# Attention and gated FFN on one core: output rows of the later batches stored as one transfer for each 32 rows

## The chip, the cores and the metric

The kernel runs on one core of one Trainium2 chip. The metric is the device time of one execution, in microseconds (us); lower is better. The kernel before took 1076.05 us (median of three runs, 1075.31 to 1076.84). The profile is of a separate execution that took 1074.98 us, of which the recorded span, from the first instruction to the last, is 1073.2 us.

Engine names in the profile: PE is the matrix engine (PEld its weight loads), DVE the vector engine, ACT the scalar engine, POOL the GpSimd engine. SP is the sync engine; it computes nothing and issues DMA transfers. A name with a q at its end (SPq, ACTq) is an engine's instruction queue: the issue of a transfer, or a wait. L498 means line 498 of the kernel's file.

## The reference

Two stages. A linear attention without softmax (8 batches, 8 heads, 576 positions, head size 64), each head's output row divided by its root mean square; then a gated feed-forward layer over all 4608 rows of 512 numbers.

```python
kv  = np.einsum('bhsd,bhse->bhde', k, v)
out = np.einsum('bhsd,bhde->bhse', q, kv)
rms = np.sqrt(np.mean(out * out, axis=-1, keepdims=True) + 1e-06)
x   = (out / rms * g_norm).transpose(0, 2, 1, 3).reshape(4608, 512)
gate = 1.0 / (1.0 + np.exp(-(x @ w_gate)))     # 512 -> 1536
val  = x @ w_val
y    = gate * val @ w_out                      # 1536 -> 512
```

The output is 4608 rows of 512 float32 numbers, 2 KB a row, 9.44 MB in all.

## The kernel before

The rows are worked on in nine chunks of 512 rows (c = 0 to 8). A chunk goes through a first layer (gate and value), then a second layer. While chunk c is in its first layer, the attention of batch c+1 is fed into the free slots between its matrix products. All tensors are float32.

The chunk's rows don't stand in memory order. Attention leaves the positions of a batch in an order that suits its transposes, and the store puts them back. For batches 0 and 1 the rows of a tile go to every sixth row of the output, in runs of up to 96. For batches 2 to 7 the order is finer: position s = 192 r + 6 p + 2 g + i, with p from 0 to 31. A group of 32 neighbouring rows of a tile has one (i, r, g) and all 32 p; up to three groups with the same i and r follow each other.

```python
QB = 32; NJ = 6; JH = NJ // 2; XC = QB * JH     # XC = 96
def sg_tile():
    return sb.tile([P, G], FP32, tag="sg", name="sg", bufs=5)     # five buffers, [128, 512]

def store(c, t, ot, cols=slice(0, DM), queues=(nc.sync,)):
    r0 = i = 0
    while r0 < P:                                     # P = 128 rows of the tile ot
        b, s = divmod(G * c + P * t + r0, S)
        rows = out[S * b:S * b + S, cols]
        if b < 2:
            j, p = divmod(s, NP)
            n = min(P - r0, NP - p)
            queues[i % len(queues)].dma_start(        # L492
                out=rows.rearrange("(p j) d -> j p d", j=NJ)[j, p:p + n], in_=ot[r0:r0 + n, cols])
        else:
            half, c0 = divmod(s, S // 2)
            r, c0 = divmod(c0, XC)
            n = min(P - r0, XC - c0)                  # 32, 64 or 96 rows
            queues[i % len(queues)].dma_start(        # L498
                out=rows.rearrange("(r p g i) d -> i r g p d", p=QB, g=JH, i=2)[
                    half, r, c0 // QB:(c0 + n) // QB],
                in_=ot[r0:r0 + n, cols])
        r0 += n
        i += 1
```

A 128-row tile so takes two transfers (96 and 32 rows, or 64 and 64). The second layer of a chunk ends with its four stores and then, on the same queue (SP), the loads of k and v for the batch that is two ahead. The tiles that are stored come from the same five buffers as those that the first layer of the next chunk writes:

```python
def second_layer_fast(c):                             # chunks 1 to 7
    ...                                               # (cut: products, L893 and L952)
    store(c, 2, o2[0])
    split(o1, d1, a2, sa2, b2, tw2_, lambda: store(c, 3, o2[1]))
    for g in pair:
        store(c, g, o1[g])
    load_late(c + 2)                                  # L114, L119: k and v, then used by feed

def first_layer_fast(c):
    ...
        def p1_out(d):
            d["u"] = d["sg"] = sg_tile()
            nc.scalar.copy(out=d["sg"][:, h2], in_=d["pa"])   # L741, on ACT
        ...
            small(pd[:, q1], tw2[2], s2[:, 1], False)
            nc.scalar.copy(out=g2[:, q1], in_=pd[:, q1])      # L801, on ACT
            small(one["pa"][:, q2], tw2[4], ax[:, 1, q2], False)   # L732, on PE

def feed(b):
        def kv_mm():                                  # L354, L360, on PE: the first use of k and v
            ...
```

Chunk 8 has a second layer of its own (L1003) in two rounds, g = 0 and 1. In the second its result is stored by column parts as they become ready, the last two parts of 128 columns over both issuing engines:

```python
            store(c, 2 + g, o2)                       # 128 x 512
            ...
            for (i_c, pc), x in zip(pcs, parts):      # parts: two of 128 columns
                give(i_c)
                product(pc, lambda f: s4[c, f][:, t1], b[2, 2][:, :, x], False)
                y = slice(DH + x.start, DH + x.stop)
                tt(out=o1[:, y], in0=pc, in1=o1[:, y], op=ALU.add)      # L1037, on DVE
                if last:
                    store(c, g, o1, y, (nc.sync, nc.scalar))
```

The framework gives every transfer one of eight completion semaphores in turn. A transfer waits, before it is issued, until the one that had its semaphore before has landed.

Of the kernel before, what the change touches and what calls it, by code (L numbers as in the profile page):

```python
# [20 lines left out]
def kernel(  # L21
# [16 lines left out]
    P = 128  # L38
# [3 lines left out]
    JH = NJ // 2  # L42
# [8 lines left out]
    QB = 32  # L51
# [3 lines left out]
    XC = QB * JH  # L55
# [427 lines left out]
    def store(c, t, ot, cols=slice(0, DM), queues=(nc.sync,)):  # L483

        r0 = i = 0
        while r0 < P:
# [5 lines that stand above are left out]
                queues[i % len(queues)].dma_start(out=rows.rearrange("(p j) d -> j p d", j=NJ)[j, p:p + n],  # L492
                                                  in_=ot[r0:r0 + n, cols])
            else:
                half, c0 = divmod(s, S // 2)
                r, c0 = divmod(c0, XC)
                n = min(P - r0, XC - c0)
                queues[i % len(queues)].dma_start(  # L498
                    out=rows.rearrange("(r p g i) d -> i r g p d", p=QB, g=JH, i=2)[half, r, c0 // QB:(c0 + n) // QB],
                    in_=ot[r0:r0 + n, cols])  # L500
            r0 += n
            i += 1
# [97 lines left out]
    for token in order.split():  # L600
        name = token.rstrip("0123456789.")
        n = [int(i) for i in token[len(name):].split(".")]
# [283 lines left out]
    def second_layer_fast(c):  # L886
# [95 lines left out]
        split(o2, d1, a4, sa4, b4, tw4)  # L982
# [5 lines that stand above are left out]
# [90 lines left out]
    for c in range(1, NG):  # L1078
        if c + 1 < B:
            steps = feed(c + 1)  # L1080
            if c == 1:

                i = 4
# [38 lines left out]
```

## Time and profile before

| | |
|---|---|
| time, median of 3 | 1076.05 us |
| span of the profile | 1073.2 us |
| PE busy | 1058.8 us, 99% |
| DVE, ACT, POOL busy | 69%, 29%, 55% |
| stores of L498 | 56 on SP, 2 on ACT |
| stores of L492 | 18 on SP |
| issue of one L498 store on SP | 0.32 to 2.26 us, median 0.70 us |
| last operation that computes | begins at 1065.46 us, takes 0.29 us |

The profile has several views. The page gives busy time by engine and the granted clock of PE in 40 slices (9 in every one: full speed). The chain of waits follows the work that ended last back in time: at each step to what released it. The list of waits tells which engine stood still and what ended it. The timeline lists instructions by start. A transfer has two times: how long its issue held the engine's queue, and when it landed, that is, when its completion semaphore was full.

### The profile page before, as it was taken

Reading aid. Unit: us, or ns where it says so; the run is one execution under the profiler, and the core shown is the slowest. Engines: PE = TensorE matmul, PEld = TensorE weight load, DVE = VectorE, ACT = ScalarE, POOL = GpSimd, SP = SyncE. Lnnn points to the kernel's source line nnn. Section 1 sums busy time; section 2 is a strip of 40 time slices with the busy share of each in tenths; the row PEclk is TensorE's granted clock in tenths of the full one; section 3 lists DMA queues with packets and bytes.
Section 4 is the critical chain, followed back from the end, with each engine's and each line's share of the span. In section 5 each row is a group of like instructions: output and inputs, shape, how many; then the busy total and the mean of one; then the engine's idle time right before and its main releaser. Section 6 shows DMA issues by size and latency. Waiting matters only on the chain.

```text
span 1073.2 us, 20591 instructions
## 1 busy us (share of the span) xinstructions
PE 1058.8 (99%) x7766; PEld 887.6 (83%) x7766; DVE 740.8 (69%) x1545; ACT 308.0 (29%) x737; POOL 587.6 (55%) x966
## 2 busy tenths in 40 slices
PE   9999999999999999999999999999999999999997
PEld 8544448888988888889888988889888988898886
DVE  4887767995678557874778557956787478738841
ACT  4654323231233113330333124311432122102210
POOL 0000036877367917783668537792778277847700
PEclk9999999999999999999999999999999999999999
DMA  9944710002400231012301140024001200010001
GB/s 271 242 157 157 244 29 23 13 13 56 140 12 13 54 103 41 23 35 48 114 13 42 28 139 13 14 55 118 22 24 25 52 10 1 1 27 14 1 1 39
DMA packets 69122, 65.03 MB, mean 61 GB/s; under 512 B 23712, under 2 KB 63008, under 8 KB 69024
## 3 DMA queue, kind: packets, MB, share of 16 engines
q1 hardware_dynamic: 68768, 63.69, 21.0%
q8 instruction: 62, 1.02, 0.4%
q14 instruction: 36, 0.29, 0.1%
q10 hardware_dynamic: 256, 0.03, 0.1%
HBM read 47.19 MB, written 9.44 MB: 53 GB/s over the span
## 4 chain that ended last, share of the span: by engine, by line
PE 95%; DMA 4%; SPq 0%; issue 0%; ACT 0%; DVE 0%; ACTq 0%
PE mm L728 45%; PE mm L893 17%; PE mm L556 7%; PE mm L732 7%; PE mm L952 5%; PE mm L653 4%; PE mm L1003 3%; DMA out_dram<-sg 3%; PE at L395 2%; PE at L354 1%; PE at L556 1%; PE two L261 1%; DMA kv<-in_v_dram 1%; PE two L291 0%; DMA v<-in_v_dram 0%; PE mm L634 0%
## 5 line engine op out<-in xcount | busy, mean ns | idle before, releaser
L720 POOL TENSOR_TENSOR tw<-gv 128x256 f32<-128x256 f32 x192 | 158.7, 836 | 258.6 <-DVE w L202 144.6
L728 PE MATMUL mm<-xT,tw 128*128 128x256 f32 x768 | 199.5, 382 | 0.0
L728 PE MATMUL mm<-sx,tw 128*128 128x256 f32 x768 | 197.5, 380 | 0.0
L720 POOL TENSOR_TENSOR tw<-gv,tw 128x256 f32<-128x256 f32 x192 | 153.5, 819 | 0.0
L728 PEld LDWEIGHTS mm<-xT,tw 128*128 128x128 f32 x768 | 136.6, 190 | 19.4 <-issue 3.8
L728 PEld LDWEIGHTS mm<-sx,tw 128*128 128x128 f32 x768 | 134.9, 191 | 12.4
L808 POOL TENSOR_TENSOR sg<-sg 128x256 f32<-128x256 f32 x48 | 35.1, 732 | 168.5 <-ACT sg L807 168.5
L775 DVE TENSOR_TENSOR gv<-gv,sg 128x256 f32<-128x256 f32 x192 | 110.9, 596 | 0.0
L741 ACT COPY sg<-mm 128x256 f32<-128x256 f32 x96 | 36.0, 375 | 248.8 <-PE mm L728 242.1
L728 PE MATMUL mm<-xT,gv 128*128 128x256 f32 x384 | 90.8, 379 | 0.0
L728 PE MATMUL mm<-sx,gv 128*128 128x256 f32 x384 | 90.7, 379 | 0.0
L766 ACT ACTIVATE sg<-sg 128x256 f32<-128x256 f32 x96 | 39.9, 415 | 149.5 <-DVE sg L765 149.4
L728 PEld LDWEIGHTS mm<-sx,gv 128*128 128x128 f32 x384 | 73.0, 190 | 9.9
L728 PEld LDWEIGHTS mm<-xT,gv 128*128 128x128 f32 x384 | 72.3, 190 | 10.0 <-issue 0.5
L556 PE MATMUL mm<-xT,gv 128*128 128x512 f32 x176 | 77.4, 594 | 0.0
L893 PE MATMUL mm<-w,s 128*128 128x256 f32 x336 | 73.7, 379 | 0.0
L893 PEld LDWEIGHTS mm<-w,s 128*128 128x128 f32 x336 | 63.8, 190 | 8.7
L751 DVE TENSOR_TENSOR gv<-mm,sg 128x256 f32<-128x256 f32 x96 | 40.0, 416 | 42.2 <-PE mm L728 41.3
L556 PEld LDWEIGHTS mm<-xT,gv 128*128 128x128 f32 x176 | 32.6, 190 | 37.4 <-issue 35.9
L747 DVE TENSOR_TENSOR gv<-mm,sg 128x256 f32<-128x256 f32 x96 | 36.6, 412 | 39.1 <-PE mm L728 32.1
L765 DVE TENSOR_TENSOR sg<-mm,sg 128x256 f32<-128x256 f32 x96 | 40.5, 421 | 33.0 <-PE mm L728 32.9
L713 POOL TENSOR_TENSOR tx<-gv,tx 128x128 f32<-128x128 f32 x96 | 54.6, 568 | 7.5
(156 smaller groups left out, 1908.5 us busy)
## 6 DMA issues: line engine op xcount, KB each, us to landing
q<-in_q_dram SPq DMA_DIRECT2D x24, 288.0 KB
st<-in_moe_w_gate_dram SPq DMA_DIRECT2D x12, 512.0 KB
st<-in_moe_w_val_dram SPq DMA_DIRECT2D x12, 512.0 KB
st<-in_moe_w_out_dram SPq DMA_DIRECT2D x12, 512.0 KB
kv<-in_k_dram SPq DMA_DIRECT2D x24, 256.0 KB
kv<-in_v_dram SPq DMA_DIRECT2D x24, 256.0 KB
out_dram<-sg SPq DMA_DIRECT2D x23, 192.0 KB
xT<-xTs SPq DMA_DIRECT2D x48, 72.0 KB
```

Of the source, the lines that this page charges most:

```text
L556: nc.tensor.matmul(self.ps[i], w[("wg", "wv")[i], self.f][:, m, :], xT[self.c][:, m, :], start=(m == 0), stop=(m == NMT - 1), skip_group_c ...
L653: nc.tensor.matmul(ps[t], gv[0, f][:, P * t:P * t + P], w["wo", f], start=(f == 0), stop=(f == NFT - 1), skip_group_check=True)
L713: nc.gpsimd.tensor_tensor(out=tw2[i], in0=in0, in1=tw2[in1] if isinstance(in1, int) else in1, op=ALU.subtract)
L720: nc.gpsimd.tensor_tensor(out=tw[f, i], in0=b[in0], in1=b[in1] if isinstance(in1, tuple) else tw[f, in1], op=ALU.subtract)
L728: nc.tensor.matmul(ps, wt[:, m, :], xs[:, m, :], start=(new and m == 0), stop=(m == NK - 1), skip_group_check=True)
L732: nc.tensor.matmul(ps, wt, xs, start=new, stop=True, skip_group_check=True)
L751: tt(out=d["h"][:, h2], in0=ps, in1=d.pop("u")[:, h2], op=ALU.add)
L765: tt(out=d["sg"][:, h2], in0=d["pb"], in1=d["sg"][:, h2], op=ALU.add)
L766: nc.scalar.activation(out=d["sg"][:, h2], in_=d["sg"][:, h2], func=AF.Sigmoid)
L775: tt(out=d["h"][:, h], in0=d["h"][:, h], in1=d["sg"][:, h], op=ALU.mult)
L893: nc.tensor.matmul(ps, hs[f], ws[:, f, :], start=(new and f == 0), stop=(f == NF2 - 1), skip_group_check=True)
L952: nc.tensor.matmul(ps, hs[j], ws[j], start=(new and j == 0), stop=(j == N3 - 1), skip_group_check=True)
```

## The change

The second branch of the store always takes one group of 32 rows. A 128-row tile of batches 2 to 7 so takes four transfers of 32 rows instead of two of 32 to 96. On both sides of a transfer the outermost dimension is now 32 rows; before, that of the output side was the number of groups, 2 or 3. The bytes, their places in memory and the order of the tiles stay as they were.

```diff
             else:
+
                 half, c0 = divmod(s, S // 2)
                 r, c0 = divmod(c0, XC)
-                n = min(P - r0, XC - c0)
+                n = QB
                 queues[i % len(queues)].dma_start(
-                    out=rows.rearrange("(r p g i) d -> i r g p d", p=QB, g=JH, i=2)[half, r, c0 // QB:(c0 + n) // QB],
+                    out=rows.rearrange("(r p g i) d -> i r g p d", p=QB, g=JH, i=2)[half, r, c0 // QB],
                     in_=ot[r0:r0 + n, cols])
             r0 += n
             i += 1
```

No instruction of PE, DVE or POOL is added, removed or moved. L498 is line 499 in the changed kernel, and so on below it.

## The prediction

> **What bounds the kernel now.** I read the page first: busy times, then the chain that ended last.
>
> ```profile
> PE 1058.8 (99%) x7766; PEld 887.6 (83%) x7766; DVE 740.8 (69%) x1545; ACT 308.0 (29%) x737; POOL 587.6 (55%) x966
> ...
> PE 95%; DMA 4%; SPq 0%; issue 0%; ACT 0%; DVE 0%; ACTq 0%
> PE mm L728 45%; PE mm L893 17%; PE mm L556 7%; PE mm L732 7%; PE mm L952 5%; PE mm L653 4%; PE mm L1003 3%; DMA out_dram<-sg 3%; PE at L395 2%; PE at L354 1%; PE at L556 1%; PE two L261 1%; DMA kv<-in_v_dram 1%; PE two L291 0%; DMA v<-in_v_dram 0%; PE mm L634 0%
> ```
>
> PE bounds the kernel. A change that touches no product can win only from the 1073.2 - 1058.8 = 14.4 us in which PE does nothing. That total caps the gain. But the chain shows stores, "out_dram<-sg", with 3%, so some of the 14.4 us belongs to them. Where do they lie? The timeline of the end comes next (start, duration, engine, line; the number before x is a count).
>
> ```profile
> 1062.58 2.84 PE L1003 MATMUL mm<-w,s 128*128 128x128 f32 x24
> ...
> 1063.23 3.25 SPq L498 DMA_DIRECT2D out_dram<-sg  x4
> ...
> 1064.44 1.66 ACTq L498 DMA_DIRECT2D out_dram<-sg  x2
> 1065.46 0.29 DVE L1037 TENSOR_TENSOR sg<-mm,sg 128x128 f32<-128x128 f32 x1 [1.05 <-PE mm L1003]
> ```
>
> All computing ends at 1065.75 (1065.46 + 0.29), the span at 1073.2: a tail of 7.45 us in which only the last stores land. Inside the kernel, PE's gaps after the start-up (longer than 0.1 us) are seven: 0.39, 1.13, 0.59, 0.96, 0.51, 0.50 and 0.22 us, together 4.3 us. The chain names what ended the larger ones (start, duration, what). Around 385 us:
>
> ```profile
> 385.38 8.54 DMA out_dram<-sg
> 393.92 0.03 ACTq L741
> 393.94 0.04 issue
> 393.99 0.37 ACT sg L741
> 394.36 0.18 ACT sg L801
> ```
>
> and around 624 us:
>
> ```profile
> 624.42 10.82 DMA out_dram<-sg
> 635.24 0.02 issue
> 635.26 0.02 SPq L114
> 635.28 0.03 issue
> 635.30 5.67 DMA kv<-in_v_dram
> ```
>
> A store that takes 8.54 us keeps one of the five sg buffers; ACT cannot write it, and PE waits 1.13 us for ACT. A store of 10.82 us keeps a completion semaphore, so the last large v load is issued only at 635.30. PE needs k and v from 638.95 on and stands for 0.96 + 0.51 us. The same happens as at 385 us once more at 739.75 (0.50 us). ACT's and PE's own lines say it:
>
> ```profile
> 393.99 0.37 ACT L741 COPY sg<-mm 128x256 f32<-128x256 f32 x1 [2.63 <-DMA out_dram<-sg]
> ...
> 394.58 0.49 PE L732 MATMUL mm<-xT,tx 128*128 128x128 f32 x2 [1.13 <-ACT sg L801]
> ```
>
> So late stores cost PE 1.13 + 0.96 + 0.51 + 0.50 = 3.1 us inside, and up to 7.45 us at the end.
>
> **What the Trainium skill says.** "DMA: Bandwidth & Descriptors", section "Why a DMA increments its semaphore by 16 and not by 1": a transfer issued by SP or ACT is not always spread over all 16 DMA engines. The outermost dimension (not of size 1) of each side is taken, and the largest number up to 16 that divides both is the number of engines; they are the lowest-numbered ones. For a store of three groups the output side has 3 outermost and the tile side 96, so 3 engines; for two groups 2; for one group 32 and 32, so 16. The same section says that the issuing side writes 16 minus that number to the semaphore at once and each engine adds one. The trace agrees: among the semaphore updates it records, every three-group store has 4 updates, every two-group store 3 and every single-group store 16. The landing times agree too. Counted from the end of issue to the last update, a three-group store of full rows takes 5.58 us at least, one of two groups 4.71, one of a single group 1.28. It also explains why a single-group store is sometimes slow (median 6.53 us): its packets stand behind the long ones on the lowest engines. The same page's section "Queues, rings and completion order" says that on each engine the queue is worked off in order. The trace shows this: a store of 32 rows issued at 615.88 landed at 622.26, 0.18 us after the three-group store issued before it.
>
> **The change part by part.** In the program, the transfers of the later batches go from 58 to 116, each with a third or half of the bytes, or the same. No compute instruction moves.
>
> 1. Issue on SP. Where nothing delays it, the issue of a single group takes 0.32 us, of two 0.53, of three 0.73, and 0.05 us pass between two. A 128-row tile costs 0.32 + 0.05 + 0.73 = 1.10 us before and 4 x 0.32 + 3 x 0.05 = 1.43 us after. That is 0.33 us more a tile and 1.3 us more a chunk of four. SP is seldom on the chain, and this lies under PE's work except at the very end.
>
> 2. Landing of the stores inside. Single groups over 16 engines should land about 1.3 to 1.9 us after issue, in place of 5 to 11. The semaphore of a store is then free long before its next turn: eight issues at 0.37 us take 3.0 us, more than 0.32 + 1.3. The sg buffer that ACT wanted at about 391.4 and got at 393.9 was stored by a transfer issued at 385.38; it should be free by about 388. The wait for it goes, and with it 1.13 and 0.50 us on PE. The stores of the chunk around 620 us finish issuing at about 623 (the last DVE addition ends at 619.75 by the timeline, then eight single stores at 0.37 us) instead of 625.16, and the k and v loads neither queue behind stores nor wait for their semaphores. In the trace, once the stores had drained, these loads landed one each 0.7 us. Eight of them and four small ones should land by about 632, well before 637.80, where PE first wants them. So 0.96 + 0.51 us go. Sum inside: 3.1 us. The remaining gaps (0.39, 0.59, 0.22) have no store in their cause and I leave them.
>
> 3. The tail. The last tile of four groups is ready at 1065.75. Before, one store of 96 x 128 numbers over three engines was issued in 0.70 us, landed at 1072.19 and 1.0 us later the span ended. It was late less because of its own bytes than because of the three-group store of full rows at 1063.60, which landed at 1070.57 on the same engines. After: both SP and ACT issue two single stores, 0.32 + 0.05 + 0.32, ready at 1066.46. SP has at 1063.23 four stores of full rows to issue and then two of the first part; that ends at about 1063.23 + 6 x 0.37 = 1065.45, before the last part is ready. Landing after 1.3 us: 1067.8. The same 1.0 us to the end: 1068.8 in place of 1073.2. Gain 4.4 us.
>
> Sum: 4.4 + 3.1 = 7.5 us. I take 0.5 us off, because something else often waits just behind a wait that is removed. 1076.05 - 7.0 gives **1069.0 us**.
>
> **The rivals.** First, SP becomes the hindrance: twice as many issues, all ahead of the k and v loads on one queue. For it: the loads came late at 638.95, and 1.3 us more a chunk is as large as the gaps. Against it: SP spent up to 2.26 us on issuing one single-group store while the queues were full (at 622.11), seven times what it takes when free; most of its time is such waiting. If landings did not improve, five chunks would lose up to 1.3 us each and the time would be about 1080. Second, eight completion semaphores for sixteen stores a chunk: if each still took 7 us to land, sixteen would take two rounds of 7 us, and the k and v loads would be several us later in five chunks, 1080 to 1090. The 1.28 us of a lone single-group store speaks against it. Third, the writes are limited by memory and not by the spread: then nothing moves, 1076. Against it: a 128-row tile in two and three groups moved at about 60 GB/s in the tail, while the first of the page's 40 slices reaches 271. Fourth, the inside gains nothing, since gaps are replaced by others (the x rows through SP, the vector engine), and only the tail wins: 1071.6.
>
> **Range and chances.** Both parts full: 1068.5. Only the tail: 1071.6. A tail somewhat shorter still, and PE's small delays below 0.1 us also gone: 1067. The runs before scatter by 0.8 us to each side. The range is 1067.0 to 1072.3. Faster by over 2% would mean below 1054.5, more than all of the 14.4 us that PE is not busy: chance 0.01. Slower by over 2% would need the semaphore rival at its worst, over 1097: 0.01. Within 2%: 0.98.
>
> **What would show it.** After, all stores of L499 should have 16 semaphore updates and land within about 2 us; the chain should no longer have 8 us pieces of "out_dram<-sg"; the wait of ACT L741 for a store (6.2 us over six times) should vanish; the gaps at about 393, 639 and 740 us should close; and the end should follow the last DVE operation by about 3 us instead of 7.45. I am wrong if landing stays near 7 us, if SP's issue time between the end of a second layer and the first k load grows beyond 3.5 us and the k and v gap widens, or if new gaps open in the first layer.

## The result and the profile after

The changed kernel took 1067.55 us (median of four runs, 1066.82 to 1069.17), the kernel before, measured with it, 1076.44 us (four runs). The ratio is 0.9918, with a 95% interval from 0.9899 to 0.9937: 8.9 us less. The predicted time was 1069.0 us and the range 1067.0 to 1072.3.

The first thing to look at is again the chain of waits on the page, here of the changed kernel (shares of the span by engine, then by line):

```profile
span 1066.2 us, 20718 instructions
...
PE 98%; DMA 1%; SPq 1%; issue 0%; DVE 0%
PE mm L729 47%; PE mm L894 17%; PE mm L557 7%; PE mm L733 7%; PE mm L953 6%; PE mm L654 4%; PE mm L1004 3%; PE at L395 2%; PE at L354 1%; DMA v<-in_v_dram 1%; PE at L557 1%; PE two L261 0%; PE two L291 0%; PE two L318 0%; PE two L272 0%; SPq L87 0%
```

"out_dram<-sg", 3% before, is gone from the chain, and so are the k and v loads of the later batches. What is left of DMA in it is the first v load of the start. The chain begins at the last operation that computes, so the tail is not in it: the 3% before were three landings inside (8.54, 10.82 and 7.97 us), and PE worked through most of that time. The timeline of ACT where it waited 2.63 us for a buffer (start, duration; in brackets the idle time before and what ended it):

```profile
391.52 0.37 ACT L742 COPY sg<-mm 128x256 f32<-128x256 f32 x1 [26.47 <-PE mm L729]
392.61 0.27 ACT L795 COPY sg<-mm 128x128 f32<-128x128 f32 x1 [0.71 <-PE mm L733]
392.77 0.38 ACT L742 COPY sg<-mm 128x256 f32<-128x256 f32 x1
393.92 0.27 ACT L802 COPY sg<-mm 128x128 f32<-128x128 f32 x1 [0.77 <-PE mm L733]
```

The second copy of L742 now has no bracket: its buffer was free. Here ACT only waits for PE, and in the list of all its waits no store is left (6.2 us, six times before). PE at the first use of k and v:

```profile
637.71 2.08 PE L354 MATMUL at<-kv 128*64 128x64 f32 x64
639.73 0.46 PE L360 MATMUL at<-kv 64*64 64x64 f32 x16
640.12 1.13 PE L729 MATMUL mm<-xT,tw 128*128 128x256 f32 x4
```

All 64 products run in one piece. And the end:

```profile
1060.36 3.68 SPq L499 DMA_DIRECT2D out_dram<-sg  x8
1061.24 0.29 DVE L1038 TENSOR_TENSOR sg<-mm,sg 128x128 f32<-128x128 f32 x1 [0.91 <-PE mm L1004]
1061.57 2.13 ACTq L499 DMA_DIRECT2D out_dram<-sg  x4
1062.59 0.29 DVE L1038 TENSOR_TENSOR sg<-mm,sg 128x128 f32<-128x128 f32 x1 [1.05 <-PE mm L1004]
```

Computing ends at 1062.88 us and the span at 1066.2. All 116 changed stores have 16 semaphore updates in the trace. Those of full rows land 1.28 to 2.86 us after the end of their issue (median 1.29), where the three-group stores took 5.58 to 10.30 us and the two-group ones 4.71 to 10.85.

To see where the time comes from, I cut the span at four places that a reader can find by line: the start of the second layer of chunk 0, the start of the first layer of chunk 2, the start of the second layer of chunk 8 ("inside" is between the last two), and the end of the last DVE operation ("tail" is from there to the end). All in us.

| kernel | second layer of chunk 0 begins | inside | tail |
|---|---|---|---|
| before | 118.11 | 754.42 | 7.45 |
| changed | 119.58 | 750.13 | 3.34 |
| e1, last chunk only | 118.24 | 753.99 | 3.10 |
| e2, chunks 2 to 7 only | 122.16 | 750.64 | 7.31 |
| e3, 16 and 16 rows | 120.08 | 757.71 | 7.63 |
| e4, 17 and 15 rows | 118.93 | 780.99 | 9.61 |
| e5, tiles 0 and 1 only | 118.05 | 754.19 | 7.25 |
| e6, tile 2 only | 118.75 | 750.06 | 7.71 |
| e7, loads first | 118.84 | 764.80 | 7.45 |
| e8, last tile over both queues | 118.85 | 749.92 | 3.14 |

So the changed kernel gains 754.42 - 750.13 = 4.3 us inside and 7.45 - 3.34 = 4.1 us at the end, together 8.4 us. The two profiles differ by only 7.0 us (1073.2 and 1066.2) because the changed kernel's profiled execution happened to be about 1.4 us slower before anything that is changed. The first column shows that this part differs from run to run by up to 4 us with the same program up to there.

### The profile page after: what moved, and what is told of

It reads as the page before. It is cut to its first block, busy times and chain, and to the rows that moved or that the text cites. A ratio compares the mean times of both kernels' runs of the same rounds, so it can differ in the third digit from the quotient of the medians.

```text
span 1066.2 us, 20718 instructions
## 1 busy us (share of the span) xinstructions
PE 1058.0 (99%) x7766; PEld 887.8 (83%) x7766; DVE 740.6 (69%) x1545; ACT 307.2 (29%) x737; POOL 587.5 (55%) x966
## 4 chain that ended last, share of the span: by engine, by line
PE 98%; DMA 1%; SPq 1%; issue 0%; DVE 0%
PE mm L729 47%; PE mm L894 17%; PE mm L557 7%; PE mm L733 7%; PE mm L953 6%; PE mm L654 4%; PE mm L1004 3%; PE at L395 2%; PE at L354 1%; DMA v<-in_v_dram 1%; PE at L557 1%; PE two L261 0%; PE two L291 0%; PE two L318 0%; PE two L272 0%; SPq L87 0%
## 5 line engine op out<-in xcount | busy, mean ns | idle before, releaser
L742 ACT COPY sg<-mm 128x256 f32<-128x256 f32 x96 | 36.0, 375 | 242.7 <-PE mm L729 238.8
```

## The experiments

All ratios are to the kernel before, with 95% intervals. The edits are to the kernel before unless said otherwise.

**e1 and e2: the two halves alone.**

```diff
-                n = min(P - r0, XC - c0)
+                n = QB if c == NG - 1 else min(P - r0, XC - c0)   # e1
+                n = QB if c < NG - 1 else min(P - r0, XC - c0)    # e2
```

> Only the stores of the last chunk (c = 8) go 32 rows at a time; chunks 2 to 7 store as before. My theory: the gain has two parts that don't touch each other. The tail from the end of the last DVE operation to the end of the span falls from 7.4 us to about 3.3 us, the gaps of PE at about 393, 639 and 740 us stay, and the time is 4.1 us under the kernel before: about 1072.3 us. Rival that the tail alone carries the gain (the gaps inside would be replaced): the whole 8.9 us, about 1067.5.

> Only the stores of chunks 2 to 7 go 32 rows at a time; the last chunk stores as before. My theory: the gaps of PE at about 393, 639 and 740 us close, worth about 4.3 us between the first layers of chunks 2 and 8; the tail stays at about 7.4 us; about 1072 us. Rival that the tail alone carries it: 1076, no gain.

e1 took 1070.35 us, ratio 0.9956 (0.9942 to 0.9970); e2 1071.22 us, ratio 0.9959 (0.9947 to 0.9971). The shortfalls from 1 add up to 0.44% + 0.41% = 0.85% (4.7 and 4.4 us, where I had expected 4.1 and 4.3); the whole change has 0.82%. In e1 the tail is 3.10 us and PE's gaps at about 393, 639 and 740 us are still there (1.09, 0.64 + 0.63 and 0.50 us). In e2 these are closed and the tail is 7.31 us. The two parts are separate and of about the same size; the rival that the tail carries all is out.

**e3 and e4: what makes a store fast, its size or its spread.** Both cut each 32-row group in two. The number of transfers is the same, and their sizes differ by one row.

```diff
-                n = min(P - r0, XC - c0)
+                n = 16 if c0 % QB == 0 else QB - c0 % QB          # e3; in e4: 17
...
-                    ...i=2)[half, r, c0 // QB:(c0 + n) // QB],
+                    ...i=2)[half, r, c0 // QB, c0 % QB:c0 % QB + n],
```

> Each group of 32 rows is cut once more, into transfers of 16 and 16 rows: eight transfers a tile, each with a number of rows that 16 engines divide. My theory: every store has 16 semaphore updates and still lands within about 2 us of its issue, but SP now issues 32 stores a chunk at about 0.47 us, so the first k load goes out about 7 us later than with 32-row stores and PE stands for k and v for 1 to 3 us in some of the five chunks; the tail grows by about 1 us. About 1069 to 1078 us, so roughly as before or a little better. Rival that a smaller transfer is what makes stores fast: better than the changed kernel, under 1067.

> The same number of transfers and almost the same sizes as with 16 and 16 rows, but 17 and 15: 17 is divided by no number up to 16 but 1, 15 by 15. My theory (the spread over DMA engines decides): a 17-row store has 2 semaphore updates, one of 15 rows 16; one engine carries 18 of each 32 rows and the stores of a tile land only after some 10 us, those of a chunk after 30 us or more; loads of k and v queue behind them on that engine, and PE stands for them in each of five chunks. Over 1100 us, with a tail of over 15 us. Rival (number and size of the transfers decide, not their spread): within 2 us of the 16 and 16 kernel.

e3 took 1078.0 us, ratio 1.0025 (1.0015 to 1.0034), e4 1105.34 us, ratio 1.0282 (1.0262 to 1.0303). Between the two the only difference is one row more here and less there, and it costs 27 us. In e3 every store has 16 updates, and those of full rows land 1.23 to 3.29 us after the end of their issue (median 1.25, with 32 rows 1.29). In e4 the 17-row stores have 2 updates (one from the issuing side, one from an engine), and those of full rows land at a median of 5.56 us. The chain of waits of e4 after the second layer of chunk 4 shows how they pile up (start, duration, what):

```profile
629.11 5.95 DMA out_dram<-sg
635.06 0.02 issue
635.08 5.79 DMA out_dram<-sg
640.87 0.02 issue
640.88 5.79 DMA out_dram<-sg
646.67 0.02 issue
646.69 5.81 DMA out_dram<-sg
```

Each link is a store that waits for the landing of the one eight before it, which has its semaphore. One pair of 17 and 15 rows lands each 1.45 us (636.50, 637.96, 639.42 and so on). The Trainium skill ("DMA: Bandwidth & Descriptors", section "Why a DMA increments its semaphore by 16 and not by 1") gives 1 engine to the one and 15 to the other, the lowest-numbered ones, so the first engine carries 18 rows of 2 KB of each pair: 36.9 KB in 1.45 us, about 25 GB/s. In the kernel before, the two-group stores landed at 627.38, 629.93 and 632.51, one each 2.55 us; two engines carry them, 65.5 KB each: 26 GB/s. It is the same limit: one engine's rate. For the landing the spread decides, not the size or the number.

The amounts of my theory for e4 were too large: a chunk's stores landed 25.6 us after the first issue (627.06 to 652.69), the tail is 9.61 us and not over 15, and PE stands for k and v in four chunks, not in five. Nor are the 27 us waits alone. Around its longest waits (up to 3.80 us) PE's granted clock falls to 0.50 in e4, for 10.2, 6.8 and 6.8 us, in which PE is busy for 20.0 us. In e3 there is one such piece of 3.4 us (644.5 to 647.9), before and in the changed kernel there is none inside. As an estimate from these times, half the clock costs 10 us in e4 and 1.7 us in e3.

Size and number do cost, on the issuing side, and e3 shows this. The wait list of PE in e3 has k and v as its first entry, where the kernel before has 1.5 us in two waits (engine, line, who ended it: us in total, times, longest):

```profile
PE at L354 <- DMA kv<-in_v_dram: 3.9, 3, 1.5
```

With 32 stores a chunk, the first k load goes out 8.6 to 11.7 us after the first layer's start in the four later chunks, against 3.3 to 4.5 us in the changed kernel. Inside, e3 loses 3.3 us to the kernel before, about half of it by that estimate to the lower clock. I had expected about 1 us more of tail than the changed kernel has, 3.34 us; it is 7.63 us. SP has 16 stores to issue from 1068.44 on, at 0.42 us and a gap each and three of them after a wait for a semaphore, and its last issue begins at 1076.31, 5.35 us after computing ended at 1070.96. So the first rival of the prediction, SP as a hindrance, is real, only not at four stores a tile.

**e5 and e6: which store causes which gap.**

```diff
-                n = min(P - r0, XC - c0)
+                n = QB if c < NG - 1 and t < 2 else min(P - r0, XC - c0)    # e5
+                n = QB if c < NG - 1 and t == 2 else min(P - r0, XC - c0)   # e6
```

> In chunks 2 to 7 only the stores of tiles t = 0 and 1, the last two of each chunk, go 32 rows at a time; t = 2 and 3, which are stored first, and chunk 8 as before. My theory of two separate waits: ACT waits at L741 for the buffer of tile t = 2, whose store is not changed here, so PE's gaps of 1.1 us at about 393 us and 0.5 us at about 740 us stay; the k and v loads no longer stand behind the stores of t = 0 and 1 and their semaphores, so the gap at about 639 us closes. Rival of one common cause (all the queue's backlog together): all three shrink alike.

> In chunks 2 to 7 only the stores of tile t = 2, the first of each chunk, go 32 rows at a time. My theory: the gaps at about 393 and 740 us, where ACT waits for that tile's buffer, close; the gap at about 639 us shrinks, as one of four tiles' backlog before the k and v loads is gone, but the semaphore of the last large v load is still held by the three-group store of t = 1, so some of it may stay, 0 to 1 us. Rival of one common cause: the gaps at 393 and 740 us stay in part, since t = 3, 0 and 1 still load the same engines.

Each ran once. In e5, with tiles 0 and 1 split, k and v are in time, but ACT and PE wait for the buffer as before. The timelines of ACT and of PE of e5:

```profile
394.51 0.37 ACT L741 COPY sg<-mm 128x256 f32<-128x256 f32 x1 [2.60 <-DMA out_dram<-sg]
```

```profile
395.10 0.49 PE L732 MATMUL mm<-xT,tx 128*128 128x128 f32 x2 [1.10 <-ACT sg L801]
...
638.65 2.09 PE L354 MATMUL at<-kv 128*64 128x64 f32 x64
```

The gap at about 740 us even grew from 0.50 to 1.72 us; why stays open. Two gaps at L395 that the profile gives to no store were 1.00 and 1.18 us in this run, before 0.39 and 0.59. So e5 has nearly no gain inside (754.19 us). In e6, with the first tile split alone, the gaps for the buffer are gone and some of the wait for v is left. Its PE:

```profile
636.06 1.70 PE L354 MATMUL at<-kv 128*64 128x64 f32 x48
638.62 0.69 PE L354 MATMUL at<-kv 128*64 128x64 f32 x16 [0.87 <-DMA kv<-in_v_dram]
```

So there are two waits with two causes: the buffer of the first tile stored, and the semaphore and queue ahead of the k and v loads. e6 has the whole gain inside (750.06 us) in spite of the gap of 0.87 us. Where it makes up for it can be read from the stages: the wait for k and v brings 0.83 us in e6 and 2.07 in the changed kernel, 1.24 less. But the products of L395 that took 2.59 us from start to next at about 550 us (549.68 to 552.27 before) took 1.73 us in e6 (548.80 to 550.53), 0.86 us less, and another 0.38 us came at about 822 us, which the changed kernel doesn't have. The gap at L395 stood between the 117th and the 118th of 144 products in all nine other profiles (0.59 to 1.18 us). The profile gives it to "issue", to no store, and what closes it in e6 stays open. With one run each, I take which gaps close as shown, and not the tenths of the sum.

**e7: move the loads and leave the stores.**

```diff
+        load_late(c + 2)
         for g in pair:
             store(c, g, o1[g])
-        load_late(c + 2)
```

> The kernel before, with the k and v loads of a chunk's end issued ahead of the stores of tiles t = 0 and 1; no store is split. My theory: the gap at about 639 us closes, since the loads stand behind two tiles' stores and not four; but the stores of t = 0 and 1 go out some 6 us later and hold their sg buffers longer, so that ACT waits at L741 in the second block of the first layer (about 634 us, and in the like place of each chunk) and PE with it. Time within 3 us of the kernel before. If the time falls by 2 us or more with no new gap, then only the place of the loads in the queue mattered, and not the stores' own landing.

1086.18 us in one run, 10.8 us over the median before (1075.35, measured with it). k and v are in time, and the wait moves to the sg buffers, where I expected it. The timeline of ACT in e7, after the second layer of chunk 4:

```profile
643.53 0.37 ACT L741 COPY sg<-mm 128x256 f32<-128x256 f32 x1 [6.71 <-DMA out_dram<-sg]
```

and PE's of e7:

```profile
637.88 1.03 PE L728 MATMUL mm<-sx,tw 128*128 128x256 f32 x4
644.21 0.77 PE L732 MATMUL mm<-xT,tx 128*128 128x128 f32 x2 [5.30 <-ACT sg L801]
```

The size was off: I expected up to 3 us in all, and this one gap takes 5.30 of 10.3 us that PE waits there in e7 (1.6 us before). Around its end the granted clock is 0.50 for 6.8 us besides (stretch; length; busy us and instructions of PE, PEld, DVE, ACT, POOL; clock; share of DMA; GB/s):

```profile
643.20:650.00 6.80, 5.79 (x36) 4.88 (x38) 1.99 (x5) 1.39 (x5) 1.45 (x2) 0.50 0.09 32
```

The stores of t = 0 and 1 now stand behind twelve loads, are issued at 634.17 to 636.97 and land at 640.93 to 646.23. Late issue and slow landing both hold the buffer. ACT stood for it from 636.82 on; the store that freed it was issued at 634.98 and landed at 643.51. With the changed kernel's 1.3 us from the end of issue it would, as an estimate, have landed at about 637. No run moved the loads and split the stores, so the share of each is not shown. What e7 does show is that the place of the loads in the queue was not the whole matter.

**e8: a little more off the end.** On the changed kernel:

```diff
-            store(c, 2 + g, o2)
+            store(c, 2 + g, o2, queues=(nc.sync, nc.scalar) if last else (nc.sync,))
```

> The changed kernel, and in the last round of chunk 8 the tile of full rows is stored over both issuing queues (SP and ACT) in turn, two 32-row stores on each. In the changed kernel SP is still busy with it when the last part is ready, 0.35 us late. I expect the last SP store 0.3 us nearer to the end of the last DVE operation, and the tail 3.0 us in place of 3.3; the time 0.3 us under the changed kernel, which is less than the runs scatter.

1067.0 us, ratio 0.9913 (0.9891 to 0.9936). Its timeline at the end:

```profile
1059.42 3.32 SPq L499 DMA_DIRECT2D out_dram<-sg  x6
1059.42 3.39 ACTq L499 DMA_DIRECT2D out_dram<-sg  x6
```

The last part is ready at 1061.93 and SP issues its first store at 1061.96, with no delay. In the changed kernel it was ready at 1062.88 and SP came to it at 1063.26. The tail is 3.14 us in place of 3.34. But e1, which ends with the code of the changed kernel, had 3.10, and the intervals of the two ratios nearly coincide. A gain over the changed kernel is not shown.

## Why the prediction was right

The mechanism was right in its main steps: stores over 2 or 3 engines land late; late landing holds the sg buffer of the first tile and the semaphores ahead of the loads; and the end of the span waits for them. Wrong in detail was that SP and the semaphores would be free in time at the very end (3 below). The total came out as 8.4 us by the profile and 8.9 by the medians (0.9918 has an interval of 6.8 to 10.9 us), against 7.5 before the discount and 7.0 after it. The inside was forecast 1.2 us too low and the tail 0.3 us too high; that these errors partly cancel is luck. The terms were sized as follows.

1. Issue on SP: predicted 1.43 us a tile, from an issue of 0.32 us. Measured is a median of 0.34 us for an issue after a pause and 0.42 us for each that follows directly, so 0.34 + 3 x 0.42 + 3 x 0.05 = 1.75 us. This term was too small by 0.3 us a tile. It cost nothing inside: in the four later chunks the first k load left 3.3 to 4.5 us after the first layer's start, before 3.1 to 6.0. In three of the four that is more than the 3.5 us that the prediction named, together with a wider k and v gap, as a sign of being wrong. But the gap closed: around 630 us the last of the loads landed at 634.05, 2 us later than forecast and still ahead of PE's first use at 637.71.

2. The inside: predicted 3.1 us, measured 4.3. What was mis-sized is the cost of a gap. I added up the gaps of PE, but a gap counts from the modelled end of the product before it. The timelines of PE at about 393 us, before:

```profile
392.42 1.03 PE L728 MATMUL mm<-sx,tw 128*128 128x256 f32 x4
394.58 0.49 PE L732 MATMUL mm<-xT,tx 128*128 128x128 f32 x2 [1.13 <-ACT sg L801]
```

and in the changed kernel:

```profile
393.94 1.03 PE L729 MATMUL mm<-sx,tw 128*128 128x256 f32 x4
394.81 0.38 PE L733 MATMUL mm<-xT,tx 128*128 128x128 f32 x2
```

Four such products are drawn 1.03 us long, but where nothing waits the next work starts 0.87 us after they do (393.94 to 394.81). A gap leaves out the 0.16 us between. The k and v stage before:

```profile
637.80 1.15 PE L354 MATMUL at<-kv 128*64 128x64 f32 x32
...
642.28 1.13 PE L728 MATMUL mm<-xT,tw 128*128 128x256 f32 x4
```

Measured from the start of the work before the gap to the start of the work after it, the k and v stage took from 637.80 to 642.28 before and from 637.71 to 640.12 after. That is 4.48 and 2.41 us, so 2.07 us less, where the gaps were 0.96 + 0.51 = 1.47. At about 393 us the same reading gives 394.58 - 392.42 = 2.16 against 0.87 us, so 1.29 for a gap of 1.13; at 740 us it gives 740.26 - 738.73 = 1.53 against 0.87, so 0.66 for 0.50. Together 4.0 us in place of 3.1. The 0.3 us that remain I don't assign.

3. The tail: predicted 4.4 us, measured 4.1. SP was not free when the last part was ready at 1062.88. With the 0.42 us of step 1 it was issuing until 1063.03, and the next semaphore in turn was held until 1063.19 by a store of ACT. SP's first store of that part began at 1063.26, 0.38 us after the end of the last DVE operation. The landing after the last issue, 1.1 us, and the 1.1 us from there to the end were about as predicted.

The 0.5 us that I took off for waits that might appear behind those removed was not needed. Of the rivals, the third (writes limited by memory) is refuted by e4 beside e3. The first and the second (SP's issues, the eight semaphores) cost 0.4 us of the tail in the changed kernel, and more once the number of stores is doubled or the landing is made slow, in e3 and e4. The fourth (only the tail gains) is refuted by e2.

## What to carry to other kernels

Look at the outermost dimension on both sides of a transfer before its size: a store whose two sides have only 2 or 3 as a common divisor there moves at 2 or 3 engines' rate, and everything behind it on those engines waits too. Splitting it into transfers with 16 as a divisor paid here even at twice the number of issues, as long as the issuing queue had time. The next doubling, at 0.47 us for each issue, gave the whole gain back here. And when a wait of the bounding engine is sized from a profile, take the difference of two starts, not the gap that is drawn.

## What the runs showed of the hardware

- The issue of a store of full rows on SP, among stores of one group: a median of 0.23 us with one engine (17 rows, e4), 0.33 us with 15 engines (15 rows, e4, always behind one of the former), and with 16 engines 0.42 us when it follows another directly (0.34 us after a pause), with 16 rows as with 32.
- One DMA engine moved rows of 2 KB at about 25 GB/s, in two different kernels (e4 and before).
- The granted clock of PE fell to 0.50 in some runs in which PE had stood still inside the kernel: in e7 for 6.8 us around the end of a gap of 5.30 us, in e4 for 6.8 to 10.2 us, in e3 for 3.4 us. In e7 four products of L728 then took 1.71 us from start to next (644.77 to 646.48), where 0.87 us is usual. Which waits bring it about is not shown: e5 has a gap of 1.72 us at 740 us and no such fall inside.
- The start of the kernel is not steady: the second layer of chunk 0 began between 118.05 and 122.16 us in ten profiled executions whose programs are the same up to there. The largest part I could name is e2, where PE stood 2.29 us for one of the first v loads and its granted clock was 0.50 for 3.4 us soon after (19.6 to 23.0).
